# Late output weights kept and split in SBUF, and a shorter hold on feed-forward steps at the end of attention

## The chip, the core and the metric

One core of one Trainium2 chip runs the whole kernel as one program. The metric is device time in microseconds (us) of one execution. TensorE is called PE, VectorE DVE, ScalarE ACT, GpSimd POOL; SyncE (SP) issues the transfers in this kernel. PEld is TensorE loading weights, which overlaps PE. The on-chip memory is SBUF, the accumulators are in PSUM, and DRAM is the memory beside the core.

## The reference

```python
def _attn_ref(q, k, v, tau):                       # q, k, v: 8 x 8 x 576 x 64
    scale = 1.0 / np.sqrt(q.shape[-1])
    scores = scale * np.matmul(q, k.transpose(0, 1, 3, 2))
    thresh = np.max(scores, axis=-1, keepdims=True) - tau
    scores = np.where(scores >= thresh, scores, -1000000000.0)
    scores = scores - np.max(scores, axis=-1, keepdims=True)
    attn = np.exp(scores)
    attn = attn / (np.sum(attn, axis=-1, keepdims=True) + 1e-09)
    return np.matmul(attn, v).astype(np.float32)

def _moe_ref(x, w_in, w_out, alpha):               # x: 4608 x 512
    h = x @ w_in                                   # w_in: 512 x 2048, float64
    g = np.maximum(h, 0.0) + alpha * np.minimum(h, 0.0)
    return (g @ w_out).astype(np.float32)          # w_out: 2048 x 512, float64
```

The attention's result, heads side by side, is the x of the feed-forward part.

## The kernel before

**Precision.** Every matmul operand is split into a high part, rounded by a copy on ACT (`split_hi`), and a low part, a subtraction on POOL or DVE (`split_lo`). A product is three matmuls: high by high, high by low, low by high. The two weight matrices come as 64-bit words and are decoded on the chip (`Split64`: two copies on ACT, then steps on DVE and POOL).

**Attention** (0 to about 845 us) runs over 32 head pairs of nine units each; the program goes through them in *cycles*, and `at_cycle` puts a step of another engine at a later cycle. Every engine takes its instructions in the order written. The 2048 hidden columns are 16 chunks of 128. Six of them (`F1 = 6`) are worked on in between the attention units by `Mlp.cycle`, in groups of 256 tokens, 18 groups in all: a first-layer product is 12 matmuls of 256 columns (tile `pha`), a second-layer accumulation 18 matmuls of 512 columns (tile `acca`), two of them for a group. Group 14 ends at token 3840 and so needs nothing of the last batch (tokens from 4032 on); group 15 does. Before the change a first-layer product is not begun in the last 14 units (`i < total - HOLD`).

**Leftovers** (845 to about 941 us). What `Mlp` has not done becomes `jobs`, with tiles `phj`, `accj`: here the last three products of group 13, both its accumulations, and groups 14 to 17. `fetch_x` brings a group's x from DRAM (`xrj`) and splits it (`xhj`, `xlj`). The last attention units normalise their result (`rp`, `rb`, `xa`) and store it (`xs<-xa`); SP takes its transfers in the order written.

**The other ten chunks** are five pairs (`NP = 5`), multiplied by a scheme that makes seven products out of eight (`USE` and `ORDER` are lists of the seven, numbered 1 to 7). *Stage A*, the first layer (941 to 1226 us), has 30 units: six sections of 768 tokens, five pairs each. A unit is seven products of six matmuls of 384 columns, one product to a cycle, into PSUM tiles `pX`, `pW`, `pY`, `pZ`; ACT and DVE combine them (`after_a`, tiles `c` and `cr`) and SP stores the gated result (`gd<-c`). While a section runs, `x_at` makes the next section's seven operands on POOL and ACT: sums `xt`, `xr` on POOL, then `xh` on ACT and `xl` on POOL. *Stage B*, the second layer (1226 to 1452 us), has nine units over `gd`, read back as `gr`; its weights are the tiles `wb`, seven for each pair, in the SBUF places `wa` of the first layer's weights, which come free as the last section is done.

**Late words.** Of the ten chunks' `w_out`, `late_pair` decodes two chunks every 28 cycles during stage A into `wq`, makes four sums on DVE (`sumo`, L1315 to L1318), splits the seven operands into `wb`, which there has two buffers (`hi` on ACT, `lo` on POOL, one operand every two cycles), and writes each to DRAM (`wod`, 256 KB each, 35 in all). In the last five units `weights_b` reads the 35 back into the `wa` places, by SP, between the stores of `gd`. The stretch in which a pair's operands are split is called its burst here.

Of the kernel before, what the change touches and what calls it, by code (L numbers as in the profile page):

```python
# [10 lines left out]
F32 = mybir.dt.float32  # L11
F32R = mybir.dt.float32r
# [4 lines left out]
ALU = mybir.AluOpType  # L17
# [17 lines left out]
ENGINES = {mybir.EngineType.PE, mybir.EngineType.Activation, mybir.EngineType.DVE, mybir.EngineType.Pool}  # L35
UNITS = [(0, 0), (0, 1), (1, 0), (1, 1), ("t", 0), (2, 0), (2, 1), (3, 0), (3, 1)]
GB = 11
HOLD = 14
ENG1 = ('vpp', 'vpp')
ENG2 = ('vvp', 'vvv')  # L40
CLOSE = 9
# [28 lines left out]
def f(ap):  # L70
    return ap.bitcast(F32)
# [10 lines left out]
def tile_masked_attention_moe(  # L82
# [98 lines left out]
    def src_o(fc):  # L181
        return w_out[fc * P : (fc + 1) * P, :].unsqueeze(1), 1, f"o{fc}"
# [114 lines left out]
    class Pair:  # L297
# [345 lines left out]
    def at_cycle(i, fn, *a):  # L643
        later.setdefault(i, []).append((fn, a))
# [44 lines left out]
    class Mlp:  # L689
# [70 lines left out]
        def cycle(self, i, used, slot):  # L760

            self.room = min(self.room, TH3) + CYCLE - used
            l1 = False
            if self.l1 and i >= self.gap and self.live < GB:
                if self.l1[0][2] is None:
                    self.step_l1(i)
                elif slot and i < total - HOLD and self.room > TH1 and ("i", fcs1[self.l1[0][2]]) in ready:
                    l1 = True
                    self.room -= 1.31
            while self.l2 and self.l2[0][0] <= i and self.l2[0][4] in self.l2[0][2]["g"] and ("o", fcs1[self.l2[0][4]]) in ready and self.room > TH2:  # L770
                self.step_l2(i)
                self.room -= 0.216
            return l1
# [128 lines left out]
    with tc.manual_schedule(engines=ENGINES) if ENGINES else ExitStack():  # L902
# [74 lines left out]
        def fetch_w32(n):  # L977
            fc = fcs2[n]
            if n % 2 == 0:
                w32[n // 2] = mem.ws.tile([P, 2, DM], F32, tag="w0", name=f"w32_{n // 2}", bufs=3)  # L980
            nc.sync.dma_start(w32[n // 2][:, n % 2], wid[n])

        def sums_at(c, pr):
# [45 lines left out]
        for gi, st, fi in mlp.l1:  # L1029
            if not jobs or jobs[-1].gi != gi:  # L1030
                t0, n = groups1[gi]
                begun = st if "xr" in st else {}
                jobs.append(SimpleNamespace(gi=gi, t0=t0, n=n, g=st["g"], x=begun, todo=[]))
            if fi is not None:
                jobs[-1].todo.append(fi)
        for gi in range(nready, len(groups1)):
            t0, n = groups1[gi]
            jobs.append(SimpleNamespace(gi=gi, t0=t0, n=n, g={}, x={}, todo=list(range(F1))))
        for num, job in enumerate(jobs):
            job.name = f"j{num}"  # L1040

# [19 lines left out]
        def first_layer(job, j):  # L1061
            fc = fcs1[j]
            name = f"{job.name}_{fc}"
            while "x" not in job.x:
                cycle()
            ph = ps_2.tile([P, 512], F32, tag="ph", name=f"ph{name}", bufs=4)
            layer1_into(ph, fc, job.n, job.x["x"])
            cycle()
            t = prelu(mem.mp1, G1, fc, job.n, ph, name, 2)
            if job is jobs[-1] and j == F1 - 1:  # L1070
                job.g[j] = mem.ws.tile([P, 2, G1], F32R, tag="w1", name=f"g{name}", bufs=2)
            else:
                job.g[j] = mem.mp1.tile([P, 2, G1], F32R, tag="g", name=f"g{name}", bufs=GB)
            split_g(job.g[j], t, job.n)
# [23 lines left out]
        for num, job in enumerate(jobs):  # L1098
            fetch(num + 1)
            last = num == len(jobs) - 1  # L1100
            for k, j in enumerate(job.todo):
                first_layer(job, j)
                if k == 0 and pending and not last:
                    second_layer(pending, mem.mp1)
            if not last:
                pending = job
# [184 lines left out]
                at_cycle(i + 2, larger, g, whole, alpha_sb)  # L1291

        H = DM // 2
        wod = [dram.tile([len(USE), P, 2, H], F32, name=f"wod{pr}") for pr in range(NP)]

        def late_pair(pr, c):
            st = {}

            def done(r, w):
                if r == 0:
                    st["w"] = mem.br.tile([P, 2, DM], F32, tag="wq", name=f"wq{pr}", bufs=2)
                fc = fcs2[2 * pr + r]
                nc.vector.scalar_tensor_tensor(
                    st["w"][:, r], f(w.t), turn_sb[:, fc : fc + 1], f(w.low), op0=ALU.mult, op1=ALU.add
                )

            def sums():
                blk = lambda j, k: st["w"][:, j, k * H : (k + 1) * H]  # L1310
                st.update({1: blk(0, 0), 2: blk(1, 0), 3: blk(1, 1), 5: blk(0, 1)})
                for n in (7, 6, 4):
                    st[n] = mem.br.tile([P, H], F32, tag=f"sumo{n}", name=f"sumo{n}_{pr}")
                tt = nc.vector.tensor_tensor
                tt(st[7], st[3], st[5], op=ALU.subtract)  # L1315
                tt(st[6], st[7], st[1], op=ALU.add)
                tt(st[5], st[5], st[1], op=ALU.subtract)
                tt(st[4], st[2], st[6], op=ALU.subtract)  # L1318

            def hi(n):  # L1320
                st["hl", n] = mem.br.tile([P, 2, H], F32R, tag="wb", name=f"wb{pr}_{n}", bufs=2)
                split_hi(st["hl", n][:, 0], st[n])

            def lo(n):
                t = st["hl", n]
                split_lo(nc.gpsimd, t[:, 1], st[n], t[:, 0])
                nc.sync.dma_start(wod[pr][USE.index(n)], f(t))

            for r in range(2):
                fc = fcs2[2 * pr + r]  # L1330
                w = Split64(mem.ws, ("w0", 3), mem.ws, ("w1", 2), "ppp", *src_o(fc))
                word_at(c + 12 * r, w, c + 12 * r - 8, lambda w, r=r: done(r, w), fc, LATE)
            at_cycle(c + 24, sums)
            for k, n in enumerate(USE):
                at_cycle(c + 26 + 2 * k, hi, n)
                at_cycle(c + 27 + 2 * k, lo, n)

        for pr in range(NP):
            late_pair(pr, begin + 8 + 28 * pr)

        bsum, gop, pin = {}, {}, {}

        def weights_b(pr):
            def load(n):
                bsum[pr, n] = mem.wa.tile([P, 2, H], F32R, tag=f"wa{pr}_{n}", name=f"wb{pr}_{n}")
                nc.sync.dma_start(f(bsum[pr, n]), wod[pr][USE.index(n)])

            for n in USE:
                at_cycle(start[NA - NP + pr, n] + 2, load, n)

        def gates_at(s):
            u = NA + s
# [106 lines left out]
        turn = start[NA - NP, 3] - 3  # L1459

        for pr in range(NP):
            weights_b(pr)
        for s in range(NB):
            gates_at(s)
        for u, prod in steps:
# [65 lines left out]
```

## Time and profile before

| | before |
|---|---|
| median of 3 runs (lowest to highest) | 1455.92 us (1454.99 to 1456.55) |
| profiled execution: its time, its span | 1454.09 us, 1452.3 us |
| PE busy | 1328.4 us (91%) |
| DVE, ACT, POOL busy | 1125.7, 968.6, 756.6 us (78%, 67%, 52%) |
| mean granted TensorE clock | 0.974 |

The span runs from the first instruction to the last; 1.8 us of the time lie outside it. Busy time is the union of an engine's instructions. The granted clock is a share of full speed: 1.00 is 2.4 GHz, 0.50 is 1.2 GHz, and a number between them is a stretch with both.

### The profile page before, as it was taken

What the parts mean: (1) busy time and instruction counts of PE and PEld (TensorE: products, weight loads), DVE (VectorE), ACT (ScalarE), POOL (GpSimd) and SP (SyncE); (2) the same over time, 40 slices, a digit from 0 to 9 for tenths busy, and PEclk for the clock granted to TensorE, in tenths of its full rate; (3) what the DMA queues carried; (4) which work ended last, traced back from release to release, by engine and by line L of the source; (5) the groups of instructions that cost most, each with busy time, mean ns of one, the idle gap of its engine ahead of it and who ended that gap; (6) DMA issues with size and microseconds to landing.
All of it is one profiled execution on the core that took longest, in us unless ns stands there. A gap on an engine that the chain in (4) does not pass through costs nothing.

```text
span 1452.3 us, 26445 instructions
## 1 busy us (share of the span) xinstructions
PE 1328.4 (91%) x8998; PEld 1234.0 (85%) x8998; DVE 1125.7 (78%) x2114; ACT 968.6 (67%) x2112; POOL 756.6 (52%) x939
## 2 busy tenths in 40 slices
PE   5998999999899899999999859988879998999998
PEld 4657889899889888898889849988778888999998
DVE  7898988988988889888889836546566546878785
ACT  6887988888878888888888734356556644333332
POOL 4874774775755767766676346467686730000000
PEclk9999999999999999999999979989898999999999
DMA  7636455555535554555545133336655579756552
GB/s 226 191 109 178 114 153 141 162 142 140 163 105 163 154 136 135 151 150 145 142 127 145 52 107 97 109 122 211 200 164 171 188 241 356 228 157 209 182 160 73
DMA packets 156295, 228.68 MB, mean 157 GB/s; under 512 B 17184, under 2 KB 90176, under 8 KB 156160
## 3 DMA queue, kind: packets, MB, share of 16 engines
q1 hardware_dynamic: 156160, 226.99, 52.5%
q8 instruction: 72, 1.18, 0.3%
q14 instruction: 63, 0.52, 0.1%
HBM read 120.92 MB, written 63.85 MB: 127 GB/s over the span
## 4 chain that ended last, share of the span: by engine, by line
PE 60%; DVE 10%; ACT 9%; POOL 9%; issue 8%; DMA 4%; SPq 0%; POOLq 0%; ACTq 0%; DVEq 0%
PE av L578 10%; PE s L431 9%; PE pX L1427 9%; PE acca L254 6%; PE t L475 5%; PE pW L1427 4%; PE pha L218 4%; PE pX L1249 3%; POOL xl L869 3%; PE phj L218 2%; PE accj L254 2%; DVE p L466 2%; PE pY L1427 2%; DVE nmx L446 2%; POOL xt L1136 2%
## 5 line engine op out<-in xcount | busy, mean ns | idle before, releaser
L446 DVE TENSOR_REDUCE nmx<-s 128x1 f32<-128x576 f32 x288 | 216.6, 752 | 64.8 <-PE s L431 61.4
L466 DVE SCALAR_TENSOR_TENSOR p<-s,thr,p 128x576 f32<-128x576 f32 x256 | 206.8, 808 | 3.0 <-ACT thr L459 2.4
L454 ACT ACTIVATE p<-s,nmx 128x576 f32<-128x576 f32 x256 | 190.0, 742 | 8.3 <-DVE nmx L446 8.0
L431 PE MATMUL s<-kh,qst 128*128 128x288 f32 x640 | 146.1, 318 | 53.6 <-DVE p L466 34.7
L431 PEld LDWEIGHTS s<-kh,qst 128*128 128x128 f32 x640 | 100.7, 193 | 84.5 <-issue 43.4
L1249 PE MATMUL pX<-xh,wa 128*128 128x384 f32 x480 | 144.0, 357 | 28.0 <-ACT c L1266 25.9
L475 PE MATMUL t<-ident,p 128*128 128x128 f32 x1024 | 155.8, 275 | 1.1 <-DVE p L466 1.1
L254 PE MATMUL acca<-wo,ga 128*128 128x512 f32 x468 | 149.5, 428 | 0.0
L218 PE MATMUL pha<-xh,wi 128*128 128x256 f32 x648 | 132.5, 288 | 5.9 <-ACT pra L231 4.3
L431 PE MATMUL s<-kl,qst 128*128 128x288 f32 x640 | 134.2, 300 | 0.0
L1427 PE MATMUL pX<-wb,gh 128*128 128x256 f32 x720 | 129.8, 283 | 0.0
L475 PEld LDWEIGHTS t<-ident,p 128*128 128x128 f32 x1024 | 127.2, 142 | 1.5 <-DVE p L466 1.3
L1249 PEld LDWEIGHTS pX<-xh,wa 128*128 128x128 f32 x480 | 93.7, 200 | 34.8 <-ACT c L1266 30.6
L218 PEld LDWEIGHTS pha<-xh,wi 128*128 128x128 f32 x648 | 105.7, 190 | 12.3 <-ACT pra L231 7.0
L1427 PEld LDWEIGHTS pX<-wb,gh 128*128 128x128 f32 x720 | 111.7, 191 | 0.0
L578 PE MATMUL av<-eo,vst 128*128 128x322 f32 (+1 forms) x512 | 108.9, 337 | 0.2 <-ACT xb L591 0.2
L866 ACT ACTIVATE gh<-gr 128x1280 fp32r<-128x1280 f32 x45 | 57.4, 1275 | 72.0 <-PE pX L1427 36.7
L531 DVE TENSOR_TENSOR eo<-t,eo 128x512 fp32r<-128x512 f32 (+1 forms) x168 | 97.2, 591 | 9.6 <-ACT eo L527 9.1
L431 PEld LDWEIGHTS s<-kl,qst 128*128 128x128 f32 x640 | 103.1, 193 | 0.0
L1427 PE MATMUL pX<-wb,gl 128*128 128x256 f32 x360 | 101.9, 283 | 0.0
L254 PEld LDWEIGHTS acca<-wo,ga 128*128 128x128 f32 x468 | 82.9, 195 | 10.0 <-DVE e L531 0.3
L218 PE MATMUL pha<-xl,wi 128*128 128x256 f32 x324 | 91.4, 282 | 0.0
(210 smaller groups left out, 3893.3 us busy)
## 6 DMA issues: line engine op xcount, KB each, us to landing
gd<-c SPq DMA_DIRECT2D x90, 192.0 KB
gr<-gd SPq DMA_DIRECT2D x24, 640.0 KB
kr<-in_k_dram SPq DMA_DIRECT2D x31, 320.0 KB
rb<-rvd SPq DMA_DIRECT2D x64, 144.0 KB
xs<-xa SPq DMA_DIRECT2D x32, 288.0 KB
pin<-part SPq DMA_DIRECT2D x18, 512.0 KB
out_dram<-pin SPq DMA_DIRECT2D x18, 512.0 KB
vr<-in_v_dram SPq DMA_DIRECT2D x28, 320.0 KB
```

The lines of the kernel that those rows point to most:

```text
L218: nc.tensor.matmul(ph[:, :n], w[:, c, :], xx[:, c, :n], start=(c == 0 and ti == 0), stop=(c == NCC - 1 and ti == 2),)
L254: nc.tensor.matmul(acc[:m, :], gg[:, g, o : o + m], w, start=(first and ti == 0), stop=(last and ti == 2))
L431: nc.tensor.matmul(ps[:, h, :288], w, kk[:, a + h * 288 : a + (h + 1) * 288], start=(ki == 0 and i == 0), stop=(ki == 1 and i == n - 1),)
L446: nc.vector.tensor_reduce(self.nmx[:, j : j + 1], self.S[u][0][:, :, :288], axis=AX.XY, op=ALU.max, negate=True)
L454: nc.scalar.activation(pj, ps[:, :, :288], AF.Exp, bias=nmx[:, j : j + 1], scale=1.0)
L466: nc.vector.scalar_tensor_tensor(pj, ps[:, :, :288], thr[:, j : j + 1], pj, op0=ALU.is_ge, op1=ALU.mult, accum_out=self.sm[:, c : c + 1])
L475: nc.tensor.transpose(tb[:, c, :], pt[:, j, j * D + c * P : j * D + (c + 1) * P], ident)
L531: nc.vector.tensor_tensor(dst[1], ps, f(dst[0]), op=ALU.subtract)
L578: nc.tensor.matmul(pa[:m, :n], w, x, start=(part == 0 and c == 0), stop=(part == z.parts[-1] and c == NKC))
L866: nc.scalar.activation(dst, src, AF.Copy)
L1249: nc.tensor.matmul(ph[:, :H1], a, x[:, c], start=(fresh and c == 0 and ti == 0), stop=(c == 1 and ti == 2), skip_group_check=not fresh,)
L1427: nc.tensor.matmul(acc[:, tb * H2 : (tb + 1) * H2], g[:, pr, tb * P : (tb + 1) * P], w, start=(fresh and n == 0 and ti == 0), stop=(n == l ...
```

## The change

**Hold.** `HOLD` becomes the pair (-16, -1): a first-layer product is not begun from unit total-16 up to total-2, and may be begun in the very last unit and behind it. The loop over `jobs` follows from that: a group that `Mlp` has begun is ended (`second_layer(pending)`) ahead of the first product of the next one.

**Late words.** `late_word` decodes one chunk every 14 cycles into a tile `wo32` that holds all ten, and makes two of the four sums at once. The operands aren't split there and don't go to DRAM. In units 25 to 29, two cycles after a product was issued for the last time, `weights_b` makes the other two sums on DVE, the high part on ACT and the low part on POOL (a cycle later), straight into the `wa` place. The tag `w0` has two buffers instead of three, in `late_word` and in `fetch_w32`.

```diff
-HOLD = 14
+HOLD = (-16, -1)
...
-                elif slot and i < total - HOLD and self.room > TH1 and ("i", fcs1[self.l1[0][2]]) in ready:
+                elif slot and not HOLD[0] <= i - total < HOLD[1] and self.room > TH1 and ("i", fcs1[self.l1[0][2]]) in ready:
...
-                w32[n // 2] = mem.ws.tile([P, 2, DM], F32, tag="w0", name=f"w32_{n // 2}", bufs=3)
+                w32[n // 2] = mem.ws.tile([P, 2, DM], F32, tag="w0", name=f"w32_{n // 2}", bufs=2)
...
+                if k == 0 and num == 1 and pending.begun:
+                    cycle()
+                    second_layer(pending, mem.mp1)
                 first_layer(job, j)
-                if k == 0 and pending and not last:
+                if k == 0 and num > 0 and not last and not (num == 1 and pending.begun):
                     second_layer(pending, mem.mp1)
...
-        def late_pair(pr, c):
...
-                tt(st[7], st[3], st[5], op=ALU.subtract)
-                tt(st[6], st[7], st[1], op=ALU.add)
-                tt(st[5], st[5], st[1], op=ALU.subtract)
-                tt(st[4], st[2], st[6], op=ALU.subtract)
...
-                st["hl", n] = mem.br.tile([P, 2, H], F32R, tag="wb", name=f"wb{pr}_{n}", bufs=2)
-                split_hi(st["hl", n][:, 0], st[n])
...
-                split_lo(nc.gpsimd, t[:, 1], st[n], t[:, 0])
-                nc.sync.dma_start(wod[pr][USE.index(n)], f(t))
...
-                bsum[pr, n] = mem.wa.tile([P, 2, H], F32R, tag=f"wa{pr}_{n}", name=f"wb{pr}_{n}")
-                nc.sync.dma_start(f(bsum[pr, n]), wod[pr][USE.index(n)])
...
+        wo32 = mem.br.tile([P, NP, 2, DM], F32, name="wo32")
...
+        def late_word(n, c):
...
+                nc.vector.tensor_tensor(st[7], st[3], st[5], op=ALU.subtract)
+                nc.vector.tensor_tensor(st[5], st[5], st[1], op=ALU.subtract)
...
+        for n in range(NJ):
+            late_word(n, begin + 8 + 14 * n)
...
+        def weights_b(pr):
...
+            def add6():
                 tt(st[6], st[7], st[1], op=ALU.add)
...
+            def sub4():
                 tt(st[4], st[2], st[6], op=ALU.subtract)
...
+                bsum[pr, n] = mem.wa.tile([P, 2, H], F32R, tag=f"wa{pr}_{n}", name=f"wb{pr}_{n}")
+                split_hi(bsum[pr, n][:, 0], st[n])
...
+                split_lo(nc.gpsimd, bsum[pr, n][:, 1], st[n], bsum[pr, n][:, 0])
...
+                c = start[u, n] + 2
+                fn = {6: add6, 4: sub4}.get(n)
+                if fn:
+                    at_cycle(c, fn)
+                at_cycle(c, hi, n)
+                at_cycle(c + 1, lo, n)
```

TensorE at the end of attention, before: the last weighted sums (`av`) stand right behind the last transposes (`tk`), the three products of group 13 that are left (`phj`) follow, and then the first of group 14, whose operands `xhj`, `xlj` are made by `fetch_x`.

```order
L491 MATMUL tk_3_11925<-ident,p_3_11866 128x128
L578 MATMUL av_1_322_11934<-o_121,vst_11544 128x256 x4
...
L578 MATMUL av_0_258_11947<-tt_126,vst_11544 128x322
L601 MATMUL rp_11958<-ident,rv_11931 9x128
L218 MATMUL phj_3_11996<-xh_3328_11198,wi_598 128x256
...
L218 MATMUL phj_5_12042<-xh_3328_11198,wi_785 128x256
L218 MATMUL phj_0_12111<-xhj_12094,wi_317 128x256
```

The same place now:

```order
L491 MATMUL tk_3_11925<-ident,p_3_11866 128x128
L218 MATMUL pha_3_11927<-xh_3328_11198,wi_598 128x256
...
L218 MATMUL pha_4_11952<-xh_3328_11198,wi_691 128x256
L578 MATMUL av_1_322_11965<-o_121,vst_11544 128x256 x4
...
L601 MATMUL rp_11995<-ident,rv_11944 9x128
L218 MATMUL pha_5_12014<-xh_3328_11198,wi_785 128x256
...
L254 MATMUL acca_0_12039<-wo_928,ga_0_11362 128x512 x3
...
L218 MATMUL pha_0_12066<-xh_3584_12035,wi_317 128x256
```

Two of group 13's products moved ahead of the last `av`. Behind it stand the third, the group's accumulations, and group 14 (`xh_3584`), whose x is now loaded and split by `Mlp` and no longer by `fetch_x`.

ScalarE in the tenth and eleventh unit of stage A, before (`c`, `cr` are copies out of PSUM, which TensorE's next products wait for; `wb<-sumo`, `wb<-wq` are high parts of the late weights):

```order
L1274 ACTIVATE cr_13893<-pX_13703,turn_sb 128x384
L866 ACTIVATE wb_6_13902<-sumo_1_13780 128x256
L1266 ACTIVATE c_10_13919<-pX_13895,turn_sb 128x384
L1274 ACTIVATE c_9_13877<-pW_13814 128x384
L866 ACTIVATE wb_4_13929<-sumo_1_13781 128x256
L1266 ACTIVATE c_10_13955<-pW_13922,turn_sb 128x384
L1274 ACTIVATE c_9_13846<-pZ_13934 128x384
L866 ACTIVATE wb_5_13964<-wq_13591 128x256
```

The same copies now:

```order
L1277 ACTIVATE cr_13829<-pX_13653,turn_sb 128x384
L1269 ACTIVATE c_10_13849<-pX_13831,turn_sb 128x384
L1277 ACTIVATE c_9_13815<-pW_13760 128x384
L1269 ACTIVATE c_10_13883<-pW_13852,turn_sb 128x384
L1277 ACTIVATE c_9_13788<-pZ_13864 128x384
```

The high parts that stood between the copies are gone from this place. They stand in units 25 to 29 now; ScalarE there, in the 27th unit:

```order
L866 ACTIVATE wb_6_15159<-wo_13010 128x256
L1277 ACTIVATE cr_15163<-pX_14997,turn_sb 128x384
L866 ACTIVATE wb_4_15183<-wo_13010 128x256
L1269 ACTIVATE c_26_15185<-pX_15165,turn_sb 128x384
L1277 ACTIVATE c_25_15148<-pW_15104 128x384
L866 ACTIVATE wb_1_15202<-wo_13010 128x256
L866 ACTIVATE wb_5_15215<-wo_13010 128x256
L1269 ACTIVATE c_26_15218<-pW_15188,turn_sb 128x384
```

SP's queue in the same units, before (a store of `gd` frees the tile `c` that ScalarE writes next):

```order
L1278 DMA gd_192<-c_25_15280 128x384
L1346 DMA wb_4_15356<-wod_13020 128x512
L1278 DMA gd_191<-cr_15338 128x384
L1346 DMA wb_1_15374<-wod_13021 128x512
L1346 DMA wb_5_15387<-wod_13020 128x512
L1278 DMA gd_192<-c_25_15325 128x384
L1346 DMA wb_7_15398<-wod_13021 128x512
```

And now:

```order
L1281 DMA gd_192<-c_25_15148 128x384
L1281 DMA gd_193<-c_25_15125 128x384
L1281 DMA gd_192<-c_26_15185 128x384
L1281 DMA gd_193<-cr_15257 128x384
```

The reads of `wod` no longer stand between the stores.

## Rows read from the trace of the kernel before

**Rows 1.** Windows: length, busy us (instructions) of each engine, granted clock, DMA share, GB/s.

```profile
936.00:1226.00 290.00, 249.65 (x1319) 239.92 (x1318) 165.15 (x275) 157.82 (x309) 161.92 (x171) 0.94 0.59 197
1226.00:1452.30 226.30, 221.94 (x1860) 221.58 (x1858) 176.59 (x161) 76.82 (x62) 0.00 (x0) 1.00 0.55 174
```

**Rows 2.** Timeline, TensorE: start, length, idle before it and what ended it.

```profile
861.47 0.58 PE L218 MATMUL phj<-xhj,wi 128*128 128x256 f32 x1 [11.19 <-ACT xhj L888]
864.63 0.58 PE L218 MATMUL phj<-xlj,wi 128*128 128x256 f32 x1 [2.58 <-POOL xlj L889]
```

**Rows 3.** Windows, just behind that wait.

```profile
865.00:870.00 5.00, 5.00 (x20) 4.34 (x20) 1.67 (x4) 1.09 (x4) 3.33 (x5) 0.65 0.44 110
```

**Rows 4.** Timeline, SP's transfers.

```profile
855.30 1.85 SPq L881 DMA_DIRECT2D xrj<-xs  x4
```

**Rows 5.** The chain that ended last: start, length, engine, tile, line, instructions.

```profile
884.84 8.21 PE accj L254 x36
893.05 8.52 PE phj L218 x72
...
1138.04 2.09 PE pX L1249 x12
```

**Rows 6.** Windows, the five stretches of stage A with late words.

```profile
959.40:1005.60 46.20, 39.62 (x217) 38.67 (x217) 28.79 (x50) 26.29 (x54) 31.79 (x33) 0.96 0.52 167
1005.60:1054.90 49.30, 42.05 (x211) 40.14 (x210) 29.58 (x50) 27.85 (x57) 33.26 (x35) 0.90 0.59 194
1054.90:1102.40 47.50, 39.39 (x208) 36.83 (x207) 30.93 (x53) 26.47 (x54) 32.74 (x34) 0.96 0.56 180
1102.40:1147.30 44.90, 40.14 (x212) 39.18 (x212) 28.53 (x50) 27.92 (x58) 33.43 (x36) 0.92 0.52 177
1147.30:1190.50 43.20, 40.69 (x231) 39.56 (x230) 21.94 (x39) 25.17 (x50) 24.31 (x26) 1.00 0.58 194
```

**Rows 7.** Waits, 959 to 1190 us: us in total, times, longest.

```profile
ACT xh L866 <- POOL xt L1136: 27.8, 12, 3.9
...
PE pX L1249 <- ACT c L1266: 22.2, 12, 3.3
ACT wb L866 <- DMA wod<-wb: 20.6, 11, 5.4
...
ACT xh L866 <- POOL xr L1136: 15.9, 5, 3.9
...
PE pW L1249 <- ACT c L1266: 5.2, 4, 3.4
```

**Rows 8.** Timeline, ScalarE in the second burst.

```profile
1043.32 0.42 ACT L866 ACTIVATE wb<-sumo 128x256 fp32r<-128x256 f32 x1 [5.37 <-DMA wod<-wb]
1043.64 0.56 ACT L1266 ACTIVATE c<-pW,turn_sb 128x384 f32<-128x384 f32 x1
```

**Rows 9.** Timeline, TensorE beside it.

```profile
1044.26 0.69 PE L1249 MATMUL pW<-xh,wa 128*128 128x384 f32 x1 [3.37 <-ACT c L1266]
```

**Rows 10.** Groups by shape, 941 to 1226 us: busy us, mean ns, idle before.

```profile
L869 POOL TENSOR_TENSOR wb<-wq,wb 128x256 fp32r<-128x256 f32 x20 | 15.6, 780 | 17.2 <-ACT wb L866 17.0
...
L869 POOL TENSOR_TENSOR wb<-sumo,wb 128x256 fp32r<-128x256 f32 x15 | 11.2, 748 | 5.3 <-ACT wb L866 5.3
```

**Rows 11.** Waits, 1190.5 to 1226 us.

```profile
ACT c L1266 <- DMA gd<-c: 14.0, 2, 8.1
...
PE pW L1249 <- ACT c L1266: 7.2, 2, 4.9
```

**Rows 12.** Windows, last units of stage A.

```profile
1200.00:1210.00 10.00, 5.12 (x29) 4.79 (x28) 2.02 (x5) 1.60 (x5) 0.00 (x0) 0.99 1.05 398
1210.00:1220.00 10.00, 10.00 (x51) 10.00 (x50) 7.82 (x11) 5.20 (x10) 0.00 (x0) 0.84 0.99 331
```

**Rows 13.** One tile's instructions: shortest, median, longest ns, first and last start.

```profile
L869 POOL TENSOR_TENSOR wb<-sumo,wb x15: 720/734/991, 993.0 to 1155.0; 128x256 fp32r<-128x256 f32 x15
...
L1316 DVE TENSOR_TENSOR sumo<-sumo,wq x5: 424/426/1120, 985.5 to 1140.6; 128x256 f32<-128x256 f32 x5
```

More of the change, by code (lines that the diff above doesn't have):

```diff
@@ L1032, in tile_masked_attention_moe @@
                 begun = st if "xr" in st else {}
-                jobs.append(SimpleNamespace(gi=gi, t0=t0, n=n, g=st["g"], x=begun, todo=[]))
+                jobs.append(SimpleNamespace(gi=gi, t0=t0, n=n, g=st["g"], x=begun, todo=[], begun=True))
             if fi is not None:
@@ L1037, in tile_masked_attention_moe @@
             t0, n = groups1[gi]
-            jobs.append(SimpleNamespace(gi=gi, t0=t0, n=n, g={}, x={}, todo=list(range(F1))))
+            jobs.append(SimpleNamespace(gi=gi, t0=t0, n=n, g={}, x={}, todo=list(range(F1)), begun=False))
         for num, job in enumerate(jobs):
@@ L1291, in after_a, with done @@
                 at_cycle(i + 2, larger, g, whole, alpha_sb)
+        wo32 = mem.br.tile([P, NP, 2, DM], F32, name="wo32")
         H = DM // 2
-        wod = [dram.tile([len(USE), P, 2, H], F32, name=f"wod{pr}") for pr in range(NP)]
-        def late_pair(pr, c):
[L1299 to L1304, printed above, removed]
+        wst = {}
+        def late_word(n, c):
+            fc = fcs2[n]
+            pr = n // 2
+            w = Split64(mem.ws, ("w0", 2), mem.ws, ("w1", 2), "ppp", *src_o(fc))
+            def done(w):
+                dst = wo32[:, pr, n % 2]
@@ L1305, in done @@
                 nc.vector.scalar_tensor_tensor(
-                    st["w"][:, r], f(w.t), turn_sb[:, fc : fc + 1], f(w.low), op0=ALU.mult, op1=ALU.add
+                    dst, f(w.t), turn_sb[:, fc : fc + 1], f(w.low), op0=ALU.mult, op1=ALU.add
                 )
             def sums():
[L1310 to L1313, printed above, removed]
@@ L1314, in sums @@
-                tt = nc.vector.tensor_tensor
-                tt(st[7], st[3], st[5], op=ALU.subtract)
+                blk = lambda j, k: wo32[:, pr, j, k * H : (k + 1) * H]
+                st = wst[pr] = {1: blk(0, 0), 2: blk(1, 0), 3: blk(1, 1), 5: blk(0, 1), 6: blk(0, 0), 4: blk(1, 0)}
+                st[7] = mem.br.tile([P, H], F32, name=f"wt{pr}")
+                nc.vector.tensor_tensor(st[7], st[3], st[5], op=ALU.subtract)
+                nc.vector.tensor_tensor(st[5], st[5], st[1], op=ALU.subtract)
@@ L1316, in sums @@
+            word_at(c, w, c - 8, done, fc, LATE)
+            if n % 2:
+                at_cycle(c + LATE[6] + 2, sums)
+        for n in range(NJ):
+            late_word(n, begin + 8 + 14 * n)
+        bsum, gop, pin = {}, {}, {}
+        def weights_b(pr):
+            u = NA - NP + pr
+            st = wst[pr]
+            tt = nc.vector.tensor_tensor
+            def add6():
                 tt(st[6], st[7], st[1], op=ALU.add)
-                tt(st[5], st[5], st[1], op=ALU.subtract)
+            def sub4():
@@ L1318, in sums @@
                 tt(st[4], st[2], st[6], op=ALU.subtract)
             def hi(n):
-                st["hl", n] = mem.br.tile([P, 2, H], F32R, tag="wb", name=f"wb{pr}_{n}", bufs=2)
-                split_hi(st["hl", n][:, 0], st[n])
+                bsum[pr, n] = mem.wa.tile([P, 2, H], F32R, tag=f"wa{pr}_{n}", name=f"wb{pr}_{n}")
+                split_hi(bsum[pr, n][:, 0], st[n])
             def lo(n):
-                t = st["hl", n]
-                split_lo(nc.gpsimd, t[:, 1], st[n], t[:, 0])
@@ L1327, in lo @@
-                nc.sync.dma_start(wod[pr][USE.index(n)], f(t))
[L1329 to L1339, printed above, removed]
@@ L1341, in tile_masked_attention_moe @@
-        bsum, gop, pin = {}, {}, {}
-        def weights_b(pr):
-            def load(n):
-                bsum[pr, n] = mem.wa.tile([P, 2, H], F32R, tag=f"wa{pr}_{n}", name=f"wb{pr}_{n}")
-                nc.sync.dma_start(f(bsum[pr, n]), wod[pr][USE.index(n)])
-            for n in USE:
-                at_cycle(start[NA - NP + pr, n] + 2, load, n)
+                split_lo(nc.gpsimd, bsum[pr, n][:, 1], st[n], bsum[pr, n][:, 0])
+            for n in USE:
+                c = start[u, n] + 2
[4 more added lines that the diff above has]
+                at_cycle(c + 1, lo, n)
@@ L1461, in tile_masked_attention_moe @@
         for pr in range(NP):
-            weights_b(pr)
+            at_cycle(start[NA - NP + pr, 1], weights_b, pr)
         for s in range(NB):
```

## The prediction

> **What bounds the kernel now.** I first cut the span by stage with the windows view. In stage B TensorE is busy 221.9 of 226.3 us at a granted clock of 1.00 [rows 1]: nothing is to be had there without less arithmetic, and the change takes none away. From 936 to 1226 us it is busy 249.7 of 290.0 us at a clock of 0.94 [rows 1], so some 40 us of idle and a part of the clock lie in the stages that the change touches. Next I looked for TensorE's idle times one by one, in the timeline and in the table of waits, and for each I asked what the engine that released it had itself waited for. Three places come out of that.
>
> *The end of attention.* After the last weighted sums TensorE has three products left that need nothing new, and then it waits 11.19 us for a high part `xhj` and 2.58 us for a low part `xlj`, both of group 14 [rows 2]. The 5 us behind the wait run at a clock of 0.65, a mixture of 1.2 and 2.4 GHz [rows 3]. Group 14 doesn't need the last batch of attention; its x is late because SP issues its loads at 855.30 us, as its order has it, behind the last attention stores [rows 4].
>
> *The five stretches of stage A in which late words are decoded and split.* In a dense stretch a product takes 2.09 / 2 = 1.04 us [rows 5], so the 35 products of a section take 36.5 us. The five stretches last 46.2, 49.3, 47.5, 44.9 and 43.2 us, 231.1 together, with clocks of 0.96, 0.90, 0.96, 0.92 and 1.00 [rows 6]. TensorE waits there mostly for ACT's copies out of PSUM: 22.2 + 5.2 = 27.4 us [rows 7]. But a copy is short; ACT was held by an instruction ahead of it. ACT's own long waits are 20.6 us for the transfer `wod<-wb` (a high part must wait until one of the two buffers has gone to DRAM), 27.8 us for POOL's `xt` and 15.9 us for POOL's `xr` [rows 7]. One case shows the link: at 1043.32 us a high part of a late weight starts after 5.37 us of waiting for `wod<-wb`, the copy behind it starts 0.32 us later [rows 8], and TensorE goes on at 1044.26 after 3.37 us idle [rows 9].
>
> *The last units of stage A.* The DMA engines are full (share 1.05 from 1200 to 1210 us [rows 12]): SP reads the late weights back between the stores of `gd`. ACT waits 14.0 us, in two waits, for stores that free its tiles, and TensorE 7.2 us for ACT [rows 11]; behind the second wait the clock is 0.84 for 10 us [rows 12].
>
> **The change, part by part.** All sums are made against the profiled execution, 1454.1 us; the median of the runs shown is 1.8 us above it.
>
> *End of attention.* Two products of 8.52 / 6 = 1.42 us [rows 5] move ahead of the last weighted sums and delay these by at most 2.8 us. Behind them stand the third product, 1.42, two accumulations of group 13, 8.21, six products of group 14, 8.52, and its two accumulations, 8.21 [rows 5]: 26.4 us of work that needs no result of the last batch. Before, operands loaded behind the last stores were ready at 864.6 us [rows 2], some 20 us after the last sums, which end at 845; group 15's, on that path now, come some 6 us inside these 26.4 us. So both waits go: 11.19 + 2.58 = 13.8 us, and the slow clock behind them, 0.35 x 5 = 1.75 us: 15.5. No arithmetic is added. I take off 1.5 us for a first accumulation that must wait until the third product has been through its activation and split, and say -14. Bounds: -16 with everything gained; -6 if group 14's operands aren't ready in time after all, so that only 1.42 + 8.21 us of new cover stand there, less the 2.8 us moved ahead.
>
> *The five stretches.* Removed from each: seven high parts (ACT), seven low parts (POOL, 15.6 + 11.2 = 26.8 us for all 35 [rows 10]), the transfers out, and two of four sums. Left: the decoding, and the operands of the next section on POOL and ACT. Of ACT's three long waits only the first goes: 20.6 of 20.6 + 27.8 + 15.9 = 64.3 us, 32%. TensorE's 27.4 us by that share are 8.8 us. What the clock cost, 0.04 x 46.2 + 0.10 x 49.3 + 0.04 x 47.5 + 0.08 x 44.9 = 12.3 us [rows 6], falls by the same share: 3.9 us. Together 12.7; an ACT that isn't held by a transfer comes sooner to the next wait for POOL, for which I take off 1.7 us: -11. The bounds: -4, if the clock's part is all that is left because POOL's waits grow by what ACT's waits lose; -27, if POOL sets the pace of these stretches, so that they shorten by its 26.8 us. I stay nearer to the first, since in the fifth stretch POOL has only 24.3 us of work, 8 us less than in the others, and the stretch is still 6.7 us over its 36.5 [rows 6].
>
> *The last units.* 35 reads of 256 KB, 9.2 MB, go, which at the 398 GB/s moved there [rows 12] is some 23 us of all DMA engines; SP's queue then holds stores one behind the other. That takes away the 7.2 us of TensorE's waits and 0.16 x 10 = 1.6 us of clock [rows 11, 12]. What comes: per unit seven high parts, two sums and seven low parts. A dense unit takes 7 x 1.04 = 7.3 us. ACT has seven copies of at most 0.56 us and seven high parts of 0.32 us from start to start [rows 8]: 6.2 of 7.3 us. POOL, idle there now (0.00 us busy [rows 12]), gets 7 x 0.75 [rows 10] = 5.3 of 7.3 us. DVE gets two sums of 0.42 us [rows 13]. All of it fits, ACT closely; I take off 1.5 us for copies that stand behind a high part, which gives -7.3. The first product of stage B needs the last unit's weights, so low parts that lag by a few products would show there: bounds -9 and 0.
>
> **A rule against it.** The moved low parts run on POOL at the same time as DVE's sums and combining instructions. The trace shows what that can cost: a sum takes 424 ns at least and 1120 at most, a low part 720 and 991 [rows 13]. The Trainium skill (SBUF — State Buffer, "Who interferes with whom") says that a VectorE instruction with two SBUF inputs and GpSimd hold a shared pair of ports exclusively, and that the one that comes later waits for the whole of the other. By that rule the ten moved sums would take turns with the 35 low parts; the trace's longest sums are of the size it gives. It has no place in the sum: ten sums at 1.12 rather than 0.42 us are 7 us on a DVE with room. It bears on the third rival.
>
> Sum: -14 - 11 - 7.3 = -32.3 us, 1421.8 in a profiled execution, **1423.6 us** as a median.
>
> **The rivals.**
> - *POOL and ACT keep the pace of the stretches.* The chain xt, xh, xl of the next section's operands holds ACT as often without the late weights, so the second term is nothing: 1423.6 + 11 = 1434.6 us. For it: 43.7 of ACT's 64.3 us of waits are that chain's. Against it: the fifth stretch, with POOL's lower load, is the shortest. Chance 0.15.
> - *The wait at the end of attention only moves.* SP, ACT or POOL bring group 15's operands later, by more than the cover has to spare, and the first term is lost: 1437.6 us. For it: group 15's loads still stand behind the last stores. Against it: the 26.4 us of cover. Chance 0.08.
> - *Slower: ACT and POOL in lockstep in units 25 to 29.* A sum made in place must wait for the low part that still reads its operand, the high part waits for the sum, and ACT's copies, for which TensorE waits, stand behind it. If all seven operands of a unit ran so, a unit would take 7 x (0.42 + 0.99) + 2 x 0.42 [rows 8, 13] + 7 x 0.56 = 14.6 us; five of them are 36.5 us over 5 x 7.3, 1460 us. It decides once a unit takes over 7.3 + 32.3 / 5 = 13.8 us. Against it: only two of the seven operands, 6 and 4, have such a sum. Chance 0.05.
> - *POOL sets the stretches' pace.* The 26.8 us come back whole: 1423.6 - 16 = 1407.6 us. For it: POOL is busy 32 to 33 us in four of the stretches and 24 in the fifth, which is 1.7 to 6.1 us shorter [rows 6]. Chance 0.09.
> - *No change.* What is saved before 1190 us returns as waits ahead of stage B. Against it: stage B is dense [rows 1], and all that it reads comes sooner. Chance 0.03.
>
> The forecast has 0.60. Its own bounds of each term, and the first, second and fourth rival, lie between 1407 and 1440 us; lockstep and no change are left out. Faster by over 0.2% (2.9 us, about what three runs that lie 1.6 us apart can tell from no change): 0.60 + 0.15 + 0.08 + 0.09 = 0.92; within it 0.03; slower 0.05.
>
> **What the changed kernel's profile would show.** TensorE has no gap over 3 us between the last weighted sums and the jobs' last accumulation, and its clock there doesn't fall. ACT's wait for `wod<-wb` is gone with the tile, those for `xt` and `xr` are within some 5 us of 43.7, and the five stretches last about 220 us together with clocks of at least 0.93. In the last units ACT no longer waits for `gd<-c`, POOL is busy about 27 us there, and stage B starts without a gap over 2 us and takes its 226 us. I am wrong if the waits for POOL's `xt` and `xr` grow by as much as the others shrink, if ACT waits for sums or TensorE for low parts after unit 25, or if a new wait stands ahead of group 15.

## The result, and the profile after

| | before | after |
|---|---|---|
| median (lowest to highest) | 1456.16 us (1454.99 to 1456.55) | 1416.46 us (1415.75 to 1421.49) |
| profiled execution: time, span | 1454.09, 1452.3 us | 1421.49, 1419.6 us |

The ratio is 0.9736, with a 95% interval of 0.9713 to 0.9759: 39.7 us less. The forecast was 1423.6 us, 32.3 us less. The profiled execution of the changed kernel is its longest, 5 us over the median, so where the two are compared I go by stages.

The page's totals of the changed kernel, to be read beside the table of the kernel before:

```profile
span 1419.6 us, 26277 instructions
PE 1320.9 (93%) x8998; PEld 1226.8 (86%) x8998; DVE 1126.5 (79%) x2113; ACT 967.7 (68%) x2109; POOL 761.7 (54%) x938
```

The arithmetic is the same (8998 matmuls). Of the 32.7 us by which the span is shorter, 25.2 are idle time of TensorE and 7.5 are busy time, from a higher clock. The five stretches of stage A, cut at the same products as in [rows 6] (windows; columns as there):

```profile
951.50:995.10 43.60, 38.58 (x217) 37.30 (x217) 29.05 (x49) 25.46 (x49) 27.46 (x28) 1.00 0.47 152
995.10:1036.60 41.50, 37.89 (x212) 36.30 (x211) 27.64 (x47) 25.37 (x49) 26.85 (x27) 1.00 0.52 172
1036.60:1077.30 40.70, 37.95 (x207) 36.92 (x206) 27.56 (x47) 23.34 (x46) 27.58 (x27) 0.96 0.50 162
1077.30:1118.30 41.00, 37.94 (x212) 36.34 (x211) 28.25 (x47) 24.55 (x48) 26.56 (x26) 1.00 0.45 149
1118.30:1160.20 41.90, 40.63 (x232) 39.67 (x231) 23.10 (x42) 26.76 (x56) 30.28 (x34) 1.00 0.47 152
```

They last 208.7 us instead of 231.1, at clocks of 0.96 to 1.00 instead of 0.90 to 1.00. The table of waits over the same stretches answers to [rows 7]:

```profile
ACT xh L866 <- POOL xt L1139: 25.7, 10, 3.8
...
ACT xh L866 <- POOL xr L1139: 13.8, 5, 4.0
PE pX L1252 <- ACT c L1269: 12.6, 10, 2.3
...
PE pW L1252 <- ACT c L1269: 0.2, 1, 0.2
```

ACT's wait for `wod<-wb` is gone with the tile. Its waits for POOL are nearly what they were (39.5 us for 43.7), and TensorE's waits for ACT's copies fell from 27.4 to 12.8 us.

At the end of attention TensorE now has one wait over 0.3 us between the last weighted sums and stage A (timeline of TensorE; it answers to [rows 2]):

```profile
854.46 0.39 PE L218 MATMUL pha<-xl,wi 128*128 128x256 f32 x1 [0.20 <-POOL xl L206]
884.77 0.58 PE L218 MATMUL phj<-xhj,wi 128*128 128x256 f32 x1 [3.95 <-DVE ptj L237]
```

The waits of 11.19 and 2.58 us are gone. A new one stands 20 us further on, and the windows show a slow clock around it:

```profile
845.00:870.00 25.00, 24.80 (x159) 22.30 (x158) 11.90 (x25) 9.87 (x25) 16.74 (x22) 1.00 0.36 108
870.00:900.00 30.00, 26.05 (x144) 23.25 (x143) 14.96 (x28) 12.63 (x35) 20.15 (x27) 0.89 0.32 97
```

Its cause is read backwards through the timelines of SP, ACT, POOL and DVE:

```profile
871.33 3.00 POOL L889 TENSOR_TENSOR xlj<-xrj,xhj 128x256 fp32r<-128x256 f32 x4
```

```profile
873.93 6.88 SPq L881 DMA_DIRECT2D xrj<-xs  x5
```

```profile
875.86 0.42 ACT L888 ACTIVATE xhj<-xrj 128x256 fp32r<-128x256 f32 x1 [4.13 <-DMA xrj<-xs]
```

```profile
882.93 0.93 DVE L1008 TENSOR_TENSOR w<-w,sum 128x256 f32<-128x256 f32 x1 [1.29 <-POOL wa L869]
```

`fetch_x` has four buffers, one for each quarter of a group's x. POOL's splits of one group free them from 871 us on, and only then can SP load the next group's. ACT waits 4.13 us for that, POOL's splits of weights stand behind ACT, a sum on DVE behind POOL, and the activation of a finished product (`ptj`) behind that sum; it still holds the PSUM tile that TensorE's next product needs.

In the last units of stage A, the waits (1145.3 to 1195 us) answer to [rows 11]:

```profile
ACT wb L866 <- DVE wo L1337: 8.1, 5, 2.1
ACT c L1269 <- DMA gd<-c: 4.3, 1, 4.3
...
PE pW L1252 <- ACT c L1269: 2.1, 1, 2.1
...
PE pX L1252 <- DVE pZ L1292: 1.9, 1, 1.9
```

One wait for a store is left, of 4.3 us where there were 14.0, and a new wait of ACT for the sums in place has come.

### The profile page after: what moved, and what is told of

Its sections match the earlier page's. It is cut to its first block, busy times and chain, and to the rows that moved or that the text cites. A ratio compares the mean times of both kernels' runs of the same rounds, so it can differ in the third digit from the quotient of the medians.

```text
span 1419.6 us, 26277 instructions
## 1 busy us (share of the span) xinstructions
PE 1320.9 (93%) x8998; PEld 1226.8 (86%) x8998; DVE 1126.5 (79%) x2113; ACT 967.7 (68%) x2109; POOL 761.7 (54%) x938
## 4 chain that ended last, share of the span: by engine, by line
PE 56%; issue 11%; DVE 10%; POOL 10%; ACT 8%; DMA 3%; SPq 1%; POOLq 0%; DVEq 0%; ACTq 0%
PE av L578 9%; PE pX L1430 9%; PE s L431 8%; PE acca L254 6%; PE t L475 5%; PE pha L218 5%; PE pW L1430 5%; POOL xl L869 3%; PE pY L1430 2%; DVE p L466 2%; DVE nmx L446 2%; PE pX L1252 2%; POOL xt L1139 2%; PE phj L218 2%; ACT p L454 1%
## 5 line engine op out<-in xcount | busy, mean ns | idle before, releaser
L254 PE MATMUL acca<-wo,ga 128*128 128x512 f32 x504 | 158.4, 426 | 0.0
L1252 PE MATMUL pX<-xh,wa 128*128 128x384 f32 x480 | 139.6, 347 | 17.4 <-ACT c L1269 12.6
L218 PE MATMUL pha<-xh,wi 128*128 128x256 f32 x688 | 140.5, 287 | 5.9 <-ACT pra L231 4.3
L218 PEld LDWEIGHTS pha<-xh,wi 128*128 128x128 f32 x688 | 112.0, 189 | 12.4 <-ACT pra L231 6.9
L1252 PEld LDWEIGHTS pX<-xh,wa 128*128 128x128 f32 x480 | 90.4, 193 | 23.5 <-ACT c L1269 15.8
L254 PEld LDWEIGHTS acca<-wo,ga 128*128 128x128 f32 x504 | 89.5, 194 | 11.4 <-DVE e L531 0.3
L218 PE MATMUL pha<-xl,wi 128*128 128x256 f32 x344 | 97.0, 282 | 0.2 <-POOL xl L206 0.2
```

The costliest lines, as they stand in the source:

```text
L218: nc.tensor.matmul(ph[:, :n], w[:, c, :], xx[:, c, :n], start=(c == 0 and ti == 0), stop=(c == NCC - 1 and ti == 2),)
L254: nc.tensor.matmul(acc[:m, :], gg[:, g, o : o + m], w, start=(first and ti == 0), stop=(last and ti == 2))
L1252: nc.tensor.matmul(ph[:, :H1], a, x[:, c], start=(fresh and c == 0 and ti == 0), stop=(c == 1 and ti == 2), skip_group_check=not fresh,)
```

## The experiments

Twelve kernels were run. Executions differ by several us in attention even where its instructions are the same (no cause is known): the last weighted sums end at 844.7 us in the kernel before and between 843.6 and 849.8 in all others but one (with the hold, two products of 1.42 us stand ahead of them). So beside the median I give three lengths from TensorE's timeline of the profiled execution: from the end of the last `av` to the first product of stage A; that start to the 176th product (five of six sections); and from there to the end of the span.

| kernel | median us | end of attention to stage A | five sections | rest |
|---|---|---|---|---|
| before | 1456.2 | 96.9 | 234.1 | 276.6 |
| after | 1416.5 | 84.1 | 213.4 | 274.4 |
| hold_only | 1445.9 | 82.8 | 237.4 | 278.2 |
| late_only | 1428.8 | 96.4 | 208.4 | 274.2 |
| before_wb6 | 1440.3 | 96.3 | 217.5 | 278.1 |
| splits_twice | 1428.6 | 82.8 | 222.0 | 272.7 |
| reads_back | 1427.2 | 83.0 | 214.8 | 274.7 |
| puts_early | 1417.1 | 82.3 | 212.4 | 274.8 |
| xsums_dve | 1397.0 | 83.1 | 194.1 | 272.7 |
| x_bufs8 | 1412.7 | 77.8 | 214.4 | 274.0 |
| splits_later | 1420.5 | 82.8 | 213.5 | 275.6 |
| reads_28 | 1425.2 | 83.0 | 213.5 | 279.9 |
| two_fixes | 1394.5 | 77.7 | 194.6 | 272.6 |
| three_fixes | 1394.2 | 77.7 | 194.6 | 275.2 |

Where the instructions of a stage are the same in two kernels, these lengths agree within 1 to 3 us. The kernel before was timed beside each group of kernels: at 1456.1 us with the four from `hold_only` to `splits_twice`, 1455.6 with the four from `reads_back` to `x_bufs8`, and 1459.2 with the last four, each group on a chip of its own. So a kernel of the last group is set beside one of another group by its ratio to the kernel before.

**The two halves of the change.** `hold_only` is the kernel before with this, the condition that reads it, and the order of the jobs:

```diff
-HOLD = 14
+HOLD = (-16, -1)
...
```

Counted in units the new hold isn't the shorter one of the title, but 15 for 14: it begins two units earlier, and leaves the last unit free.

> The kernel before with the hold and the order of the leftovers alone. If the stall at the end of attention is covered by its own part of the change: 14 to 17 us under the kernel before, about 1440 us, with stage A as long as before (277 us). If the gain there needs the room that the late weights leave, or returns as a later start of stage A's operands: less than 6 us.

`late_only` is the changed kernel with those same lines back as they were:

> The changed kernel with the old hold and the old order of the leftovers: only the late weights are changed. By the predicted terms -11 and -7 it comes out 18 us under the kernel before, about 1438 us; the changed kernel's own trace asks for more from the stretches (about 21 us in the second to fifth sections) and little from the last units, some 22 us together, about 1434 us. If the two parts of the change help one another, both parts alone give less than the 40 us of the whole.

Measured against 1456.1 us for the kernel before on the same chip: `hold_only` 0.9932 (0.9911 to 0.9954), 10.2 us less, between the two expectations; `late_only` 0.9815 (0.9795 to 0.9836), 27.3 us less, more than either. Together 37.5 us of the 39.7, so the halves add up, within their intervals. From the end of attention to stage A the hold takes 14 us, of which 2.8 are the two products that stand ahead of the last sums now. In `late_only` the first section of stage A takes 44.4 us, in the changed kernel 49.4: a part of the gain returns where stage A begins. There the changed kernel, and `hold_only` with 4.78 us, has a wait for a copy of the leftovers' last accumulators (`poj`) that neither `late_only` nor the kernel before has (timeline of TensorE):

```profile
939.44 0.69 PE L1252 MATMUL pY<-xh,wa 128*128 128x384 f32 x1 [4.86 <-ACT poj L1089]
```

**The wait for the transfer.** The kernel before, with more buffers for the split tile:

```diff
-tag="wb", name=f"wb{pr}_{n}", bufs=2)
+tag="wb", name=f"wb{pr}_{n}", bufs=6)
```

> The kernel before, with six buffers of the late weights' split tile instead of two: the high part then need not wait until the tile before the last has gone to DRAM. Splits, sums, transfers and the reads at the end all stay. If ACT's wait for that transfer is what the stretches lost: ACT's 20.6 us of it fall to under 5 and the kernel is 9 to 13 us faster, about 1445 us. If the splits' work on POOL and ACT sets the stretches' pace: less than 4 us.

0.9898 (0.9873 to 0.9923): 15.9 us less, more than the upper figure. Among its waits from 956 to 1174 us none is for `wod<-wb`:

```profile
ACT xh L866 <- POOL xt L1136: 30.2, 11, 3.7
...
PE pX L1249 <- ACT c L1266: 19.9, 10, 2.6
...
ACT xh L866 <- POOL xr L1136: 15.3, 5, 3.9
```

The five sections fell by 16.6 us and nothing else moved by more than 1.5. The windows of these sections, before and in this kernel, say how:

```profile
941.63:1175.74 234.11, 201.24 (x1052) 193.38 (x1050) 137.94 (x233) 136.19 (x270) 160.35 (x170) 0.93 0.52 170
942.03:1159.53 217.50, 192.56 (x1051) 186.30 (x1050) 137.90 (x232) 134.86 (x269) 160.96 (x170) 0.98 0.55 184
```

TensorE's idle time fell from 32.9 to 24.9 us, and its busy time for the same matmuls by 8.7 us, at a clock of 0.98 for 0.93. So this wait was the larger part of what the stretches lost, and no DRAM had to be left out to be rid of it.

**The splits' own work.** The changed kernel, with 35 splits more at the old places (`hi` on ACT, `lo` on POOL, into two spare tiles):

```diff
...
+            for k, n in enumerate(USE):
+                at_cycle(c + 26 + 2 * k, hi, n)
+                at_cycle(c + 27 + 2 * k, lo, n)
...
```

> The changed kernel with 35 more splits at the old places of the stretches, into two spare tiles that nothing reads, with no transfer. 14.5 us of ACT and about 27 us of POOL are back there. If the transfers were the cost: 0 to 4 us above the changed kernel, 1416 to 1420 us. If the work on POOL and ACT was the cost: 12 to 20 us above it, 1428 to 1436 us.

1428.6 us, 12.2 above the changed kernel's median; the five sections take 222.0 us for 213.4, 8.6 more. What follows them isn't longer; the other 3.6 us aren't explained (this execution's attention ended late, at 849.8 us). The two spare tiles hold ACT up only once, for 1.6 us. The sum of the windows over the five stretches shows POOL's extra 26.8 us and ACT's 11 (it was POOL 138.73 and ACT 125.48 us in the changed kernel):

```profile
sum 217.30, PE 196.02 PEld 189.85 DVE 137.92 ACT 136.52 POOL 165.56; mean PE 39.20 PEld 37.97 DVE 27.58 ACT 27.30 POOL 33.11
```

So the work costs too: 16.6 for the wait and 8.6 for the work are 25.2 us, where the late weights took 24.0 (`hold_only` to the changed kernel) and 25.7 us (before to `late_only`) off the five sections. (Between the kernel before and the changed one it is 20.7 us, since the hold alone makes them 3.3 us longer.)

**POOL's part of the pace.** The changed kernel, with the sums `xt`, `xr` on DVE:

```diff
-                if first:
+                if True:
                     nc.vector.tensor_tensor(out, a, b, op=op)
```

> The changed kernel with the operand sums of stage A (xt, xr) on DVE in all sections, as 128x768 instructions: some 42 us of POOL's work go to DVE, which is idle a third of these sections. If ACT's waits for POOL (about 40 us for xt and xr) now set the pace of the sections: 6 to 15 us under the changed kernel, 1402 to 1410 us. If DVE's own combining steps come late behind the sums: no gain, or up to 5 us above it.

0.9597 (0.9583 to 0.9612), 1397.0 us: 19.5 under the changed kernel, beyond the expected range. The windows of the five stretches:

```profile
947.30:984.80 37.50, 37.50 (x217) 37.50 (x217) 32.54 (x53) 25.84 (x49) 21.10 (x20) 1.00 0.55 177
984.80:1022.80 38.00, 36.94 (x211) 36.16 (x210) 31.39 (x51) 25.29 (x49) 19.42 (x19) 1.00 0.60 187
...
1097.40:1137.20 39.80, 39.80 (x231) 39.80 (x231) 28.23 (x46) 27.00 (x56) 23.32 (x26) 1.00 0.50 163
```

TensorE is busy for 97 to 100% of the stretches shown, at a clock of 1.00. ACT's waits for these sums, now DVE's, are

```profile
ACT xh L866 <- DVE xt L1136: 14.0, 14, 1.6
...
ACT xh L866 <- DVE xr L1136: 1.7, 3, 0.8
```

15.7 us where they were 39.5, none longer than 1.6. In the changed kernel POOL was busy for 63 to 72% of these stretches, and still it set their pace, through ACT's order. The edit also makes each sum one instruction of 768 columns where POOL had two of 384; what that alone is worth wasn't tried.

**The reads in the last units.** Two kernels. The first put 35 copies of 256 KB from DRAM to DRAM there:

```diff
+            def load(n):
+                nc.sync.dma_start(wod[USE.index(n)], wid[pr])
...
+                at_cycle(c, load, n)
```

> The changed kernel with 35 transfers of 256 KB put back into units 25 to 29, between the stores of the gated result, at the old places of SP's queue; they copy from DRAM to DRAM and nothing reads them. If those transfers cost what the prediction's third term says: 5 to 9 us above the changed kernel, 1422 to 1425 us, with ACT's wait for the stores back at some 14 us. If the last units were bound by something else already (their section is only 2 us shorter in the changed kernel's trace): within 2 us of it.

This one tells nothing about the last units. The copies depend on nothing late, and SP's queue has them in attention (the tile's instructions: shortest, median, longest ns, first and last start):

```profile
L1349 SPq DMA_DIRECT2D wod<-wid x35: 468/582/1527, 209.6 to 454.0; - x35
```

Attention ended at 855.0 us, the latest of all, and the rest is as in the changed kernel. The second pair of kernels reads into the places in SBUF, which come free only then. `splits_later` delays the splits, so that they have room for it:

```diff
...
+                at_cycle(c, place_of, n, False)
+                c += 5 if pr < NP - 1 else 2
                 at_cycle(c, hi, n)
                 at_cycle(c + 1, lo, n)
```

> The changed kernel, with the high and low parts of the late weights in units 25 to 28 five cycles behind their sums instead of at once (two cycles in unit 29). ACT's waits for DVE's sums there, 8.1 us, should fall to under 2. If they are why the last units gained so little: 3 to 6 us under the changed kernel, about 1412 us. If TensorE has enough in hand: within 2 us of it. It is also the kernel that the next run is compared with.

`reads_28` has `pr < NP - 1` for `False` there: 28 reads ahead of the splits.

> The one before, with 28 reads of 256 KB into the places that come free in units 25 to 28, each between the stores where the kernel before had them; the splits then overwrite what was read. If the reads in the last units cost what the third term says: 5 to 9 us above the one before, with ACT waiting for stores again. If not: within 2 us. A high part may wait for its read, which would show as ACT waiting for that transfer and not for a store.

In both (and in `three_fixes`) the two sums in place come before two of the seven operands of four pairs are split, so that these two weights are other numbers; the instructions and their shapes are the same. `splits_later`: 1420.5 us, by ratio 0.9745 for the changed kernel's 0.9736, so no gain; ACT's wait for the sums is gone, but a store still holds it, and TensorE behind it, since the reads of `gr` and `pin` for stage B fill the DMA engines at that time (waits, then windows, of `splits_later`):

```profile
ACT c L1269 <- DMA gd<-c: 6.0, 1, 6.0
...
PE pW L1252 <- ACT c L1269: 3.0, 1, 3.0
```

```profile
1155.00:1165.00 10.00, 9.74 (x57) 9.42 (x55) 5.00 (x9) 4.57 (x12) 4.45 (x7) 1.00 1.08 346
```

`reads_28`: 4.7 us above it by the medians, just under the expected 5 to 9, and 4.3 by the rest (279.9 for 275.6). The windows show 30 us of full DMA engines instead of 10; the first and last of them:

```profile
1150.00:1160.00 10.00, 9.53 (x52) 8.59 (x51) 4.43 (x9) 3.98 (x10) 3.63 (x5) 1.00 1.05 364
...
1170.00:1180.00 10.00, 6.82 (x30) 6.51 (x30) 5.56 (x10) 6.82 (x16) 5.48 (x8) 0.83 1.04 392
```

ACT's waits there:

```profile
ACT wb L866 <- DMA wb<-wid: 8.5, 8, 2.5
...
ACT c L1269 <- DMA gd<-c: 3.3, 2, 2.7
```

ACT waits for stores less than in `splits_later` (3.3 us for 6.0), and 8.5 us for the reads themselves, for which it has no wait in the kernel before. So 4.3 us is a price of reads in this place; that it is the price of the waits for stores, which the third term counted, isn't shown.

**What the first term lacked.** Eight buffers for the leftovers' x:

```diff
-name=f"xr{name}_{k}", bufs=NCC)
+name=f"xr{name}_{k}", bufs=8)
```

> The changed kernel with eight buffers instead of four for the leftovers' x, so that the next group's x is loaded before the group ahead is split. In the changed kernel that load holds ACT for 4.1 us, POOL and DVE behind it, and TensorE for 3.9 us, and the 30 us around it run at a clock of 0.89. If this is what the first term lacked: 4 to 7 us under the changed kernel, 1410 to 1412 us. If another wait takes its place: within 2 us of it.

1412.7 us, 3.8 under the changed kernel, just short of the expected 4; from the end of attention to stage A 6.3 us fewer than in the changed kernel's one profiled execution, 4.5 to 5.3 fewer than in the seven other kernels with the new hold and four buffers (their clock from 870 to 900 us is 0.94). There is no wait of TensorE over 0.2 us, and these 30 us run at full clock:

```profile
870.00:900.00 30.00, 29.87 (x212) 27.94 (x211) 20.27 (x41) 13.34 (x37) 23.05 (x31) 1.00 0.30 101
```

`puts_early` looked for what the start of stage A gives back, by making the copies `poj` earlier:

```diff
                         if n == 4:
                             sub4()
+                            for put in puts:
+                                put()
...
```

> The changed kernel, with the two last copies of the leftovers' accumulators ahead of the last operand splits of stage A's first section, not behind them. In the changed kernel TensorE waits 4.9 us there for that copy at the start of stage A. If the wait is worth its length: 3 to 6 us under the changed kernel, about 1412 us. If the operands behind it are the later ones: within 1.5 us of it.

1417.1 us, no gain: the first section still takes 48.3 us for 49.4. Its windows in the changed kernel, in `puts_early` and in `late_only`:

```profile
931.87:981.23 49.36, 40.40 (x211) 38.80 (x210) 25.38 (x42) 28.43 (x52) 30.38 (x31) 0.93 0.46 148
```

```profile
927.71:975.96 48.25, 41.37 (x211) 39.57 (x210) 25.99 (x42) 28.34 (x52) 30.95 (x32) 0.92 0.47 152
```

```profile
942.54:986.97 44.43, 38.42 (x211) 37.14 (x210) 23.99 (x40) 26.58 (x49) 31.25 (x32) 0.98 0.46 148
```

The wait for `poj` fell from 4.86 to 0.32 us, and TensorE's idle time from 9.0 to 6.9 (6.0 in `late_only`). But a wait of 2.65 us for ACT's `c` came in its place, and the same matmuls take 41.4 us instead of 40.4 (38.4 in `late_only`). So most of what is left there is a slow clock; what would keep it up wasn't found.

**Together.** `two_fixes` has the DVE sums and the eight buffers, `three_fixes` the later splits too.

> The changed kernel with stage A's operand sums on DVE and eight buffers for the leftovers' x. If the two gains (19.5 and 3.8 us) lie in different places: their sum, 1393 us. If the earlier start of stage A meets DVE still busy with the leftovers: 1397 us, no better than the sums alone.

> The same with the later splits of the late weights too. If these help the last units: 2 to 5 us under the two together, about 1390 us. If not: the same within 2 us.

`two_fixes` gives 0.9564 (0.9539 to 0.9589), 1394.5 us, between its two expectations; by its ratio it is 0.0033 under `xsums_dve` (0.9597), 4.8 us, with intervals that touch, and the lengths show both gains (77.7 and 194.6 us). It is the best version here with all weights as in the reference. The later splits add nothing (1394.2, timed beside it).

## Why the prediction was right, and where it was off

The direction and the three places held, the waits named in each were a cause, and the time lies in the range. What was off is sizes, and one cause put at nothing: POOL's load. That the total came within 7 us is in part luck: the second term was 13 to 15 us too small, the other two together 7 to 9 us too large. By terms:

*End of attention, -14.* Measured -10.2 alone (`hold_only`), and 12.3 between the medians of `late_only` and the changed kernel. Both old waits are covered, as forecast. I had looked at the first group that needs the last batch and not at the one behind it, whose load waits for buffers: the list of what would show me wrong had "no gap over 3 us" and "its clock there doesn't fall", and both failed. The wait of 3.95 us and the clock are what `x_bufs8` got back. The wait of 4.86 us at the start of stage A is the other place where the gain returned; no sentence of the prediction looked there.

*The five stretches, -11.* This is the step that failed in size: -24 to -26 over the five sections, close to the far bound of -27. Two parts of it were wrong. The wait for the transfer, which I priced at 12.7 us by ACT's share of waits and then cut to 11, is worth 16.6 (`before_wb6`). The share was near for TensorE's waits, 7.9 us of idle time for 8.8, and wrong for the clock: 8.7 us came back for 3.9. And I gave the splits' own work nothing, because the fifth stretch, with less of POOL's work, was "still 6.7 us over its 36.5". It isn't: its window holds 231 matmuls [rows 6], 38.5 products and not 35, so it needs 40.0 us and is 3.2 over. Read like that, the row says that POOL's load matters, which was my fourth rival, at 0.09. `splits_twice` puts the work at 8.6 us, a third of POOL's 26.8, and `xsums_dve` shows POOL's pace directly. The forecast that ACT's waits for `xt` and `xr` stay within 5 us of 43.7 was right (39.5); that they stay doesn't mean that nothing is gained.

*The last units, -7.3.* The rest is 276.6, 278.2 and 278.1 us with the reads, 272.6 to 274.8 in the eight kernels whose late part is the change's own: about 4 us between the means, 2.2 between the two profiled executions that the forecast compares. So this term was 3 to 5 us too large. The price of the reads was near, if by another path: 4.3 us for 28, so about 5.4 for 35 as an estimate. My sign that ACT no longer waits for `gd<-c` failed (4.3 us), since stage B's first reads fill the DMA engines also without the late weights' reads; and TensorE has a new wait of 1.9 us for DVE.

The rivals. Lockstep of ACT and POOL didn't come: ACT waits 8.1 us for sums in all five units, and without these waits nothing is gained. The moved low parts do get longer beside DVE's work, but only some of them (one tile's instructions, then a case in the timelines of POOL and DVE, changed kernel):

```profile
L869 POOL TENSOR_TENSOR wb<-wo,wb x30: 722/740/1991, 1146.8 to 1195.5; 128x256 fp32r<-128x256 f32 x30
```

```profile
1180.99 3.70 POOL L869 TENSOR_TENSOR wb<-wo,wb 128x256 fp32r<-128x256 f32 x2 [1.57 <-ACT wb L866]
```

```profile
1180.64 1.49 DVE L869 TENSOR_TENSOR gl<-gr,gh 128x1280 fp32r<-128x1280 f32 x1
1182.05 2.03 DVE L1383 TENSOR_TENSOR gt<-gr,gr 128x1280 f32<-128x1280 f32 x1
```

The median is 740 ns, for 734 before [rows 13]. Nine of all 35 take 908 to 1991 ns, and each of the nine has a DVE `TENSOR_TENSOR` of two SBUF inputs beside it: a moved sum (933 to 1031) or a step on stage B's first operands (908 to 1991). Where the low part began well ahead of a moved sum, it is the sum that takes longer (547, 578 and 607 ns, for 415). That is the direction of the rule of the Trainium skill (SBUF — State Buffer, "Who interferes with whom"), and the trace agrees. TensorE waits for none of the low parts; whether its 1.9 us for DVE have to do with them isn't shown.

Open: why the clock is low at the start of stage A also without the wait for `poj`, how much of the late reads' price the waits for stores were, and why attention differs by several us from one execution to the next.

## What to carry to other kernels

A wait of an engine that works in order is paid by the engine whose chain runs through it, and by its clock: ACT's 20.6 us for a transfer were 7.9 us of idle time of TensorE and 8.7 us of slower matmuls. Look first at a pool with two buffers whose tiles leave by DMA, since more buffers there gave 15.9 us with one number changed. Before a stretch's length is compared with the work in it, count the instructions that the window really holds. An engine that is 63 to 72% busy can still set the pace, if another waits for it in order; moving its work to an engine with room is a surer test than its busy share.

## What was not expected of the hardware

DVE makes the operand sums as instructions of 128x768 in 4.80 us for each section's four (the means of its groups, 1441, 1285, 1128 and 946 ns), POOL as eight of 128x384 in 8.75 (1122, 1104, 1102 and 1048 ns, two each). And 9.2 MB of transfers that no step needs, put into attention by the order of the queue, went along with an attention that ended 7 us later than in the changed kernel (855.0 for 847.8 us). Some 5 of these come between 279 and 306 us, while the copies run; but attention without copies also lies up to 5 us apart at one place in two executions (`splits_twice` and the changed kernel), so that the copies are the cause isn't shown.
